# Another order of the first loads in front of a gated MLP: one part of a weight matrix ahead of the second unit's queries and keys, four parts behind later values

## The chip, the cores and the metric

The kernel runs on one core of a Trainium2 chip. The metric is the device time of one execution in microseconds (us); lower is better. TensorE (PE) multiplies matrices, VectorE (DVE), ScalarE (ACT) and GpSimd (POOL) do elementwise work, and nearly all transfers are issued by SyncE (SP). Every engine works through its own list of instructions in order, and an instruction that waits holds up all that stands behind it on that engine.

## What is computed

Chunked attention over 4 batches, 8 heads, 768 tokens and a head dimension of 64, followed by a gated MLP with a product over the tokens:

```
for each chunk of 32 queries:                      # 24 chunks
    k_ctx, v_ctx = keys, values from 16 before the chunk to 8 behind it
    k_full, v_full = 8 memory rows + k_ctx, v_ctx
    a = softmax(q_c @ k_full.T / 8)
    x_c = a @ v_full
x  : (4, 768, 512)                                 # heads side by side
h  = relu(x @ w_in);  u, v = h[..., :512], h[..., 512:]
vn = (v - mean(v)) / sqrt(var(v) + 1e-6)
vs = einsum('ts,bsd->btd', w_spatial, vn) + b_spatial
out = (u * vs) @ w_out
```

All inputs are 32-bit floats but w_in and w_out, which are 64-bit floats in memory.

## The kernel before

**Units.** The attention is done in 24 units: a unit is four chunks (128 queries) of all heads of one batch, six units to a batch. Unit i needs its queries and keys (loaded for two units at a time by `load_qk(g)`; the first pair is loaded as two single units, `load_qk(0, (0,))` and `load_qk(0, (1,))`), a copy of its keys with the memory keys between them (`prep`, ACT, L404), and its values (`load_v(i)`, four transfers, each with 128 KB or 96 KB). `burst(i)` holds 64 small matmuls for the scores of unit i ("s", L419 `sx<-kmain,q`) and 64 for the product of unit i-1's probabilities with its values ("a", L419 `sx<-vmain,pT`). The softmax is three steps on DVE with an exp on ACT between: maximum (L476), subtract (L480), exp (L485), sum and reciprocal (L490 to L493). The probabilities are transposed on PE (L507) and copied (L510), the output of "a" is scaled on DVE (L459, `xs`), transposed on PE (L523, `xt`), and split into a high part (ACT, L528) and a low part (DVE, L532), the tile x.

**First product.** Each product is made of three matmuls, high times high, low times high and high times low. w_in has 512 rows (four parts of 128, c = 0 to 3) and 1024 columns in two halves: the u half (part 0) and the v half (part 1). `w_in_part(c, part, rank, load_rank, engine)` loads one such part, 512 KB of 64-bit numbers, into one of four buffers (`big`), makes 32-bit numbers of it (`from_f64`: ACT L864 and L869, DVE L873 and L874, POOL L879), and splits these into `win_h` (ACT L893) and `win_l` (L897, on DVE for the v parts and on POOL for the u parts). `ffn_v` of unit t's 128 tokens takes x of this unit and the four v parts, in order of c (L561 to L563, 128x512); `ffn_u` takes x of three units and the four u parts (L561 to L563, 128x384). So no `ffn_v` can end before all v parts are split, and no `ffn_u` before all u parts are. Results go to DRAM (`vn_far`, `u_far`) and come back for the second half of the kernel, the spatial product and the product with w_out (L710).

**Who sets the order.** Nobody writes out the order of the engines' lists. Each step is given to `Plan.op` with its engine, an assumed duration, what it reads and writes, and a rank. `Plan.order` then plays through the whole kernel by these assumed durations: of all steps that could go, the one with the earliest start is taken, on equal start the lower rank. The result is the fixed order of each engine's list. A transfer is taken to land at `max(pipe, issue) + size * drag / rate` plus `landing`, with `pipe` the end of the transfer before it: so `landing` and `drag` change no transfer, but they change when the plan believes its data to be there, and with that the order of all lists. Loads with `seq=True` keep the order of the program on SP. `alone` keeps a DVE step off planned POOL work and POOL off it. Where PE would wait in the plan between 9 and 36 us, small matmuls that nobody reads (L252, `idle`) are put in, as many as fit.

**How many transfers fly.** `held_by` sets a wait of each transfer on an earlier one, in the plan as in the kernel, so that no more than a window of megabytes is under way (and, after the first 9 MB, no more than 8 transfers): 2.0 MB for the first 9 MB, 1.2 MB up to 38 MB (`MIDDLE`), 1.75 MB behind that.

Of the kernel before, what the change touches and what calls it, by code (L numbers as in the profile page):

```python
# [10 lines left out]
U32 = mybir.dt.uint32  # L11
# [8 lines left out]
SLOT = 40  # L20
LEFT = 16
WIN = 64
MIDDLE = (38.0, 1.2)
PIECES = 4
NEG = -1.0e30

# [1 line left out]
class Plan:  # L28
# [14 lines left out]
    def op(self, eng, us, fn, r=(), w=(), rank=0.0, mb=0.0, tail=0.0, after=None, alone=False, drag=1.0, shared=False):  # L43
        n = len(self.ops)
        deps, begun = set(), set()
        if after is not None:
            begun.add(after)
        for key in r:
            deps.add(self.writer.get(key))
            self.readers.setdefault(key, []).append(n)  # L50
        for key in w:
            deps.add(self.writer.get(key))
            deps.update(self.readers.get(key, ()))
            self.writer[key], self.readers[key] = n, []
        deps -= {None, n}
        held = {k[:2] for k in (*r, *w) if isinstance(k, tuple) and k[0] in self.rings}
        for s in held:
            if s not in self.slots and s[0] not in self.loose:
                if s[0] in self.newest:
                    begun.add(self.newest[s[0]])  # L60
                self.newest[s[0]] = n
            self.slots.setdefault(s, []).append(n)
        begun -= deps
        self.ops.append((eng, us, fn, deps, rank, mb, tail, held, begun, alone, drag, shared))
        return n
# [74 lines left out]
    def held_by(self, flight, mb, none):  # L140

        moved = sum(size for _, size in flight)
        window = self.early[1] if moved <= self.early[0] else MIDDLE[1] if moved < MIDDLE[0] else self.window
        for back, (name, size) in enumerate(reversed(flight), 1):
            mb += size
            if back == 8 and moved > self.early[0] or mb > window:
                return name
        return none
# [10 lines left out]
def tile_chunked_attention_gmlp(  # L159
# [43 lines left out]

    sizes = {"f": 3, "sx": 1, "pt": 1, "xt": 1, "y": 5, "st": 9, "big": 4, "uo": 2, "x": 2, "vm": 3,
             "q": 2, "k": 2, "kT": 2, "p": 1, "xs": 1, "pT": 1, "vr": 2, "op": 4, "sm": 2, "ug": 6, "ot": 11}
    plan = Plan(sizes, {"f", "y", "st", "big", "ot"}, rate=0.30, landing=2.5, lat=0.06, window=1.75, early=(9.0, 2.0))
    op = plan.op

    def act(n):
# [56 lines left out]
    def src(t, offset, ap):  # L266
        return bass.AP(tensor=t.tensor, offset=offset, ap=ap)
# [12 lines left out]
    def transfer(e, out_, in_, mb, of=None):  # L280
        ins = e.dma_start(out=out_, in_=in_)
        made.setdefault(of, []).append(ins.ins.name)
        wait = plan.held_by(flight, mb, None)
        if wait:
            wait_for(ins, [wait], "pace")
        flight.append((ins.ins.name, mb))

    def load(dst, src_, w, rank, r=(), eng="SP", slow=1.0, us=0.45, seq=False, drag=1.0, of=None):
        e = {"SP": nc.sync, "ACT": nc.scalar, "POOL": nc.gpsimd}[eng]
        n = 4  # L290
        for s in src_.shape:
            n *= s
        mb = n / 1e6 * slow
        n = op(eng, us, lambda: transfer(e, dst() if callable(dst) else dst, src_, mb, of), r=r, w=w, rank=rank, mb=mb,
               after=line.get(eng) if seq else None, drag=drag)
        if seq:
            line[eng] = n
# [10 lines left out]
    def spot(name, g, shape):  # L308
        if (name, g) not in t_:
            alloc(name, g, shape, F32)  # L310
        return t_[name, g]

    def load_qk(g, units=(0, 1), seq=True):
        i = 2 * g
        b, c0 = i // UB, (i % UB) * UC
        off = b * H * D * S + c0 * CH
        nk = 2 * UT + CH
        lo = LEFT if c0 == 0 else 0
        hi = nk - LEFT if c0 + 2 * UC == NC else nk
        q0, q1 = units[0] * UT, units[-1] * UT + UT  # L320
        k0, k1 = max(lo, q0 + (CH if q0 else 0)), min(hi, q1 + CH)
        u = units[0]
        ks = ("k", g)
        n = PIECES if g > 1 else 1
        for t in range(n):
            ts = slice(t * T // n, (t + 1) * T // n)
            load(lambda ts=ts: spot("q", g, [P, T, 2 * UT])[:, ts, q0:q1],
                 src(q, off + q0 + ts.start * P * S, [[S, P], [P * S, T // n], [1, q1 - q0]]), w=[("q", g, u, t)], rank=10.0 * i,
                 slow=1.15, seq=seq)
        for t in range(n):  # L330
            ts = slice(t * T // n, (t + 1) * T // n)
            load(lambda ts=ts: spot("k", g, [P, T, nk])[:, ts, k0:k1],
                 src(k, off - LEFT + k0 + ts.start * P * S, [[S, P], [P * S, T // n], [1, k1 - k0]]), w=[("k", g, u, t)],
                 rank=10.0 * i, slow=1.15, seq=seq)

        def pad():
            a = t_["k", g]
            if k0 == lo > 0:
                nc.gpsimd.memset(a[:, :, 0:lo], 0.0)
            if k1 == hi < nk:  # L340
                nc.gpsimd.memset(a[:, :, hi:nk], 0.0)
        if k0 == lo > 0 or k1 == hi < nk:
            op("POOL", 0.2, pad, w=[ks + (u, "pad")], rank=10.0 * i, after=len(plan.ops) - 1)
# [203 lines left out]
    seq = [0]  # L547
# [305 lines left out]
    def from_f64(name, src_, rank, load_rank, home, after=()):  # L853
        big = ("big", *name)
        zk = ("st", ("z", name))

        def get():
            a = alloc("big", big, [P, 2 * DH], U32).rearrange("p (c w) -> p c w", w=2)
            t_[big] = a
            return a  # L860
        load(get, src_.bitcast(U32).rearrange("p (c w) -> p c w", w=2), w=[("big", big)], r=after, rank=load_rank, seq=True)

        def scale_():
            nc.scalar.activation(alloc("st", ("z", name), [P, DH], F32), t_[big][:, :, 1].bitcast(F32), AF.Copy,  # L864
                                 scale=2.0 ** -112)

        def rest():
            a = t_[big][:, :, 0]
            nc.scalar.activation(a, a, AF.Copy, scale=2.0 ** -29)  # L869

        def shift():
            zu = t_["st", ("z", name)].bitcast(U32)
            nc.vector.tensor_scalar(zu, zu, 3, None, op0=ALU.logical_shift_left)  # L873
            nc.vector.scalar_tensor_tensor(zu, t_[big][:, :, 1], 0x80000000, zu,  # L874
                                           op0=ALU.bitwise_and, op1=ALU.bitwise_or)

        def add():
            zu = t_["st", ("z", name)].bitcast(U32)
            nc.gpsimd.tensor_tensor(t_[big][:, :, 1] if home else zu, zu, t_[big][:, :, 0], op=ALU.add)  # L879
        op("ACT", 0.66, scale_, r=[("big", big)], w=[zk], rank=rank)  # L880
        op("DVE", 1.12, shift, r=[("big", big)], w=[zk], rank=rank, alone=True)
        op("ACT", 0.66, rest, r=[("big", big)], w=[("big", big, "r")], rank=rank)
        op("POOL", 1.6 if home else 1.35, add, r=[("big", big, "r"), zk] if home else [("big", big, "r")],
           w=[("big", big)] if home else [zk], rank=rank)
        if home:
            return (lambda: t_[big][:, :, 1].bitcast(F32)), ("big", big)
        return (lambda: t_["st", ("z", name)]), zk
# [14 lines left out]
    def w_in_part(c, part, rank, load_rank, sub_eng):  # L902
        cols = slice(part * DH, (part + 1) * DH)
        z, zk = from_f64(("win", c, part), w_in[c * P:(c + 1) * P, cols], rank, load_rank, False)
        split(sub_eng, DH, lambda x: (win_l if x else win_h)[:, c, cols], z, [zk], [("win", c, part)], rank)
# [64 lines left out]
    for j in range(NV):  # L970
        spread_mem(j, "DVE" if j < 1 else "POOL", 1.0 + 10 * j)
    load_qk(0, (0,))
    load_qk(0, (1,))
    w_in_part(0, 1, 5.0 + 0, 2.0 + 0, "DVE")
    w_in_part(1, 1, 5.0 + 1, 2.0 + 1, "DVE")
    w_in_part(2, 1, 5.0 + 2, 2.0 + 2, "DVE")
    w_in_part(3, 1, 5.0 + 3, 2.0 + 3, "DVE")
    load_v(0)
    load_qk(1)
    w_in_part(0, 0, 25.0 + 0, 15.0 + 0, "POOL")  # L980
    load_v(1)
    w_in_part(1, 0, 25.0 + 1, 15.0 + 1, "POOL")
    load_v(2)
    w_in_part(2, 0, 25.0 + 2, 15.0 + 2, "POOL")
    w_in_part(3, 0, 25.0 + 3, 15.0 + 3, "POOL")
    for j in range(NK):
        spread_keys(j, 1.0 + j)
    for i in range(NU + 1):
# [23 lines left out]
    for b in range(B + 1):  # L1012
        if b < B:
            rank = 300.0 + 10 * b
# [67 lines left out]
```

## Time and profile before

| | |
|---|---|
| three timed runs | 376.54, 379.18, 381.41 us (median 379.18) |
| profiled execution | 375.05 us, span 373.3 us from the first to the last instruction |
| PE busy in the span | 355.9 us (95%) |
| DVE, ACT, POOL busy | 285.0 (76%), 187.1 (50%), 160.5 us (43%) |
| granted TensorE clock, mean | 0.999 of full speed |

The busy time of PE holds the filling matmuls of L252, which are no work of the kernel. The stretches below are in us from the start of the span. A row of the timeline gives start, duration, engine, line, operation, the tile written and the tiles read, and how many; brackets give the engine's idle time before it and what ended that.

### The profile page before, as it was taken

To read this page: it belongs to the slowest core of one execution; us is meant where nothing else is said; L and a number is where in the kernel's file an instruction comes from. 1 tells how busy PE (TensorE), PEld (TensorE's weight loads), DVE (VectorE), ACT (ScalarE), POOL (GpSimd) and SP (SyncE) were. 2 spreads that over 40 slices of the span, in tenths; PEclk is the share of its full clock that TensorE was granted. 3 is DMA by queue.
4 is the path that set the end of the run, shared out by engine and by line. 5 is a ranking of instruction groups with operands and counts; after the bars stand their busy time and mean duration, and the time that the engine had idled before them with its cause. 6 is when DMAs were issued, how large, how long until landed. Compare 5 with 4: busy or idle time off the path is not lost.

```text
span 373.3 us, 11922 instructions
## 1 busy us (share of the span) xinstructions
PE 355.9 (95%) x4988; PEld 326.7 (88%) x4988; DVE 285.0 (76%) x479; ACT 187.1 (50%) x334; POOL 160.5 (43%) x155
## 2 busy tenths in 40 slices
PE   2987989999999999999999999999999999999995
PEld 2865877998988978979889898999999999999995
DVE  3888856748758568566598589999969896898893
ACT  3768435454555454554473355346434743744371
POOL 6446642374386077520042194961256025106500
PEclk9999999999999999999999999999999999999999
DMA  8995888778787765886742648205720662230014
GB/s 230 316 260 140 232 257 210 235 217 220 228 251 214 249 212 147 274 232 194 216 163 93 246 137 311 88 2 173 246 90 3 207 217 84 84 130 2 0 54 159
DMA packets 48517, 65.52 MB, mean 176 GB/s; under 512 B 5456, under 2 KB 39888, under 8 KB 48464
## 3 DMA queue, kind: packets, MB, share of 16 engines
q1 hardware_dynamic: 47808, 64.44, 56.5%
q8 instruction: 39, 0.64, 0.8%
q10 hardware_dynamic: 656, 0.33, 0.3%
q14 instruction: 14, 0.11, 0.1%
HBM read 45.88 MB, written 18.87 MB: 173 GB/s over the span
## 4 chain that ended last, share of the span: by engine, by line
PE 83%; DVE 11%; ACT 2%; issue 2%; DMA 1%; SPq 0%; ACTq 0%; DVEq 0%
PE y L710 21%; PE f L710 15%; PE f L561 12%; PE f L562 11%; PE f L563 11%; PE sx L419 9%; PE xt L523 3%; PE pt L507 3%; DVE op L690 2%; DVE sm L673 2%; DMA k<-in_k_dram 1%; DVE st L874 1%; DVE st L873 1%; DVE wout L897 1%; DVE p L480 1%
## 5 line engine op out<-in xcount | busy, mean ns | idle before, releaser
L710 PE MATMUL y<-wsp,op 128*128 128x384 f32 x288 | 52.0, 336 | 0.9 <-ACT st L750 0.9
L764 POOL TENSOR_TENSOR ug<-st,ug 128x384 f32<-128x384 f32 x24 | 36.0, 1513 | 38.4 <-DVE st L756 34.4
L710 PEld LDWEIGHTS y<-wsp,op 128*128 128x128 f32 x288 | 49.9, 188 | 1.2 <-ACT st L750 1.2
L561 PE MATMUL f<-x,win_h 128*128 128x384 f32 x128 | 46.1, 360 | 0.0
L563 PE MATMUL f<-x,win_h 128*128 128x384 f32 x128 | 43.2, 337 | 0.0
L562 PE MATMUL f<-x,win_l 128*128 128x384 f32 x128 | 43.1, 337 | 0.0
L561 PE MATMUL f<-win_h,x 128*128 128x512 f32 x96 | 40.8, 425 | 0.0
L710 PE MATMUL f<-wsp,op 128*128 128x384 f32 x216 | 39.4, 336 | 0.0
L562 PE MATMUL f<-win_h,x 128*128 128x512 f32 x96 | 37.9, 394 | 1.0 <-DVE x L532 1.0
L563 PE MATMUL f<-win_l,x 128*128 128x512 f32 x96 | 37.7, 392 | 0.0
L710 PEld LDWEIGHTS f<-wsp,op 128*128 128x128 f32 x216 | 37.6, 188 | 0.0
L690 DVE TENSOR_TENSOR op<-sm,op 128x768 fp32r<-128x768 f32 x32 | 34.7, 1093 | 3.1 <-ACT op L687 2.6
L710 PE MATMUL y<-wout,op 128*128 128x256 f32 x288 | 35.9, 281 | 0.5 <-DVE op L690 0.5
L459 DVE TENSOR_TENSOR xs<-sx,rec 128x512 f32<-128x512 f32 x24 | 16.5, 687 | 25.1 <-PE sx L419 25.0
L710 PEld LDWEIGHTS y<-wout,op 128*128 128x128 f32 x288 | 34.7, 188 | 1.0 <-DVE op L690 0.8
L770 POOL TENSOR_TENSOR st<-st,bias 128x384 f32<-128x384 f32 x14 | 18.6, 1337 | 37.2 <-ACT st L750 28.4
L597 POOL TENSOR_TENSOR rstd<-ve,mhalf 128x1 f32<-128x1 f32 x24 | 14.7, 611 | 44.7 <-DVE ve L593 43.6
L687 ACT CAST op<-sm 128x768 fp32r<-128x768 f32 x32 | 26.2, 837 | 11.6 <-DVE sm L673 10.2
L419 PEld LDWEIGHTS sx<-kmain,q 64*32 64x32 f32 x1536 | 17.0, 107 | 14.8 <-issue 11.7
L622 ACT ACTIVATE uo<-f 128x384 f32<-128x384 f32 x32 | 15.6, 492 | 25.2 <-PE f L563 21.9
L398 POOL COPY vmain<-memv 8x1024 f32<-8x1024 f32 x22 | 23.9, 1090 | 10.0 <-PE sx L419 7.8
L419 PE MATMUL sx<-kmain,q 64*32 64x64 f32 x1536 | 20.9, 228 | 7.3 <-ACT kmain L404 7.0
(86 smaller groups left out, 770.6 us busy)
## 6 DMA issues: line engine op xcount, KB each, us to landing
vmain<-in_v_dram SPq DMA_DIRECT2D x48, 128.0 KB
vn_far<-st SPq DMA_DIRECT2D x24, 256.0 KB
u_far<-uo SPq DMA_DIRECT2D x32, 192.0 KB
vr<-vn_far SPq DMA_DIRECT2D x8, 768.0 KB
ug<-u_far SPq DMA_DIRECT2D x16, 384.0 KB
q<-in_q_dram SPq DMA_DIRECT2D x40, 128.0 KB
vmain<-in_v_dram SPq DMA_DIRECT2D x47, 96.0 KB
out_dram<-ot SPq DMA_DIRECT2D x33, 128.0 KB
```

The lines of the kernel that those rows point to most:

```text
L398: ins = {"DVE": nc.vector, "POOL": nc.gpsimd}[eng].tensor_copy(to, of)
L419: ins = nc.tensor.matmul(o, w_, m, start=True, stop=True, skip_group_check=True)
L459: nc.vector.tensor_tensor(xs.rearrange("p t r d -> p r t d"), t_["sx", i][:, :, 1], rec.rearrange("p t r -> p r t").unsqueeze(3).broadcast ...
L561: nc.tensor.matmul(o, lh, rh, start=(j == 0), stop=False)
L562: nc.tensor.matmul(o, ll, rh, start=False, stop=False)
L563: nc.tensor.matmul(o, lh, rl, start=False, stop=(j == len(pairs) - 1))
L622: op("ACT", act(HT), lambda: nc.scalar.activation(alloc("uo", i, [P, HT], F32), t_["f", n], AF.Relu), r=[("f", n)], w=[("uo", i)], rank=rank)
L687: nc.scalar.copy(half(0), of())
L690: nc.vector.tensor_tensor(half(1), of(), half(0).bitcast(F32), op=ALU.subtract)
L710: nc.tensor.matmul(o, x, y, start=first and m == 1, stop=m == 3 * chunks, skip_group_check=True)
L764: nc.gpsimd.tensor_tensor(g, t_[st(x)], g, op=ALU.mult)
L770: {"DVE": nc.vector, "POOL": nc.gpsimd}[eng].tensor_tensor(a, a, bias[:, 1], op=ALU.add)
```

## The change

Six edits. (1) The v part c = 1 of w_in is loaded ahead of the second unit's q and k; the other v parts follow behind these, now in the order 0, 3, 2. (2) The u parts, before one ahead of `load_v(1)`, one ahead of `load_v(2)` and two behind it, now stand two ahead of `load_v(2)` (1, then 0) and two behind it (3, then 2), so the first one goes behind the second unit's values. (3) The rank of the u parts' conversion is 12 + c for 25 + c. (4) The plan takes a transfer to land 2.0 us behind its last byte for 2.5. (5) It takes the 64-bit loads (w_in and w_out) to need 0.8 of the time. (6) Between 9 and 10.5 MB the window is 1.75 MB for 1.2.

```diff
-MIDDLE = (38.0, 1.2)
+MIDDLE = (10.5, 38.0, 1.2)
...
-        window = self.early[1] if moved <= self.early[0] else MIDDLE[1] if moved < MIDDLE[0] else self.window
+        window = self.early[1] if moved <= self.early[0] else MIDDLE[2] if MIDDLE[0] < moved < MIDDLE[1] else self.window
...
-    plan = Plan(sizes, {"f", "y", "st", "big", "ot"}, rate=0.30, landing=2.5, lat=0.06, window=1.75, early=(9.0, 2.0))
+    plan = Plan(sizes, {"f", "y", "st", "big", "ot"}, rate=0.30, landing=2.0, lat=0.06, window=1.75, early=(9.0, 2.0))
...
-        load(get, src_.bitcast(U32).rearrange("p (c w) -> p c w", w=2), w=[("big", big)], r=after, rank=load_rank, seq=True)
+        load(get, src_.bitcast(U32).rearrange("p (c w) -> p c w", w=2), w=[("big", big)], r=after, rank=load_rank, seq=True, drag=0.8)
...
     load_qk(0, (0,))
+    w_in_part(1, 1, 5.0 + 1, 2.0 + 1, "DVE")
     load_qk(0, (1,))
     w_in_part(0, 1, 5.0 + 0, 2.0 + 0, "DVE")
-    w_in_part(1, 1, 5.0 + 1, 2.0 + 1, "DVE")
+    w_in_part(3, 1, 5.0 + 3, 2.0 + 3, "DVE")
     w_in_part(2, 1, 5.0 + 2, 2.0 + 2, "DVE")
-    w_in_part(3, 1, 5.0 + 3, 2.0 + 3, "DVE")
     load_v(0)
     load_qk(1)
-    w_in_part(0, 0, 25.0 + 0, 15.0 + 0, "POOL")
     load_v(1)
-    w_in_part(1, 0, 25.0 + 1, 15.0 + 1, "POOL")
+    w_in_part(1, 0, 12.0 + 1, 15.0 + 1, "POOL")
+    w_in_part(0, 0, 12.0 + 0, 15.0 + 0, "POOL")
     load_v(2)
-    w_in_part(2, 0, 25.0 + 2, 15.0 + 2, "POOL")
-    w_in_part(3, 0, 25.0 + 3, 15.0 + 3, "POOL")
+    w_in_part(3, 0, 12.0 + 3, 15.0 + 3, "POOL")
+    w_in_part(2, 0, 12.0 + 2, 15.0 + 2, "POOL")
```

## Rows read from the trace of the kernel before

**Rows 1.** Busy time of each engine by stretch: first PE, later DVE; last the clock.

```profile
7.00:24.20 17.20, 16.06 (x311) 12.76 (x311) 15.43 (x26) 11.24 (x20) 8.76 (x7) 1.00 1.04 310
24.20:37.40 13.20, 10.92 (x234) 8.14 (x232) 11.44 (x23) 10.01 (x18) 7.02 (x6) 1.00 0.64 173
37.40:54.50 17.10, 16.20 (x326) 14.08 (x327) 11.52 (x24) 6.32 (x12) 8.95 (x13) 1.00 0.85 246
54.50:203.00 148.50, 147.67 (x3025) 129.26 (x3023) 104.26 (x219) 77.78 (x138) 65.28 (x72) 1.00 0.72 213
```

**Rows 2.** Groups by line on PE, 7 to 37.4 us: the filling matmuls.

```profile
L252 PE MATMUL idle<-ident 128*128 128x256 f32 x44 | 11.9, 420 | 0.0
```

**Rows 3.** Timeline of PE, 6 to 38 us.

```profile
10.93 0.86 PE L419 MATMUL sx<-kmain,q 64*32 64x64 f32 x64
...
12.21 5.78 PE L252 MATMUL idle<-ident 128*128 128x256 f32 x26
...
18.36 0.86 PE L419 MATMUL sx<-vmain,pT 64*32 64x64 f32 x64
...
24.16 0.50 PE L561 MATMUL f<-win_h,x 128*128 128x512 f32 x1
...
27.13 0.86 PE L419 MATMUL sx<-vmain,pT 64*32 64x64 f32 x64
...
31.99 0.75 PE L419 MATMUL sx<-vmain,pT 64*32 64x64 f32 x51 [0.96 <-issue]
...
37.40 0.50 PE L562 MATMUL f<-win_h,x 128*128 128x512 f32 x1 [1.01 <-DVE x L532]
```

**Rows 4.** Timeline of DVE, 10 to 39 us.

```profile
10.55 0.69 DVE L490 TENSOR_REDUCE den<-p 128x8 f32<-128x512 f32 x1 [0.70 <-ACT p L485]
...
15.86 1.52 DVE L873 TENSOR_SCALAR st<-st 128x512 uint32<-128x512 uint32 x1
...
...
18.48 1.67 DVE L874 SCALAR_TENSOR_TENSOR st<-big,st 128x512 uint32<-128x512 uint32 x1
...
20.68 0.68 DVE L459 TENSOR_TENSOR xs<-sx,rec 128x512 f32<-128x512 f32 x1
...
22.86 0.68 DVE L532 TENSOR_TENSOR x<-xt,x 128x512 fp32r<-128x512 f32 x1
...
27.58 0.69 DVE L490 TENSOR_REDUCE den<-p 128x8 f32<-128x512 f32 x1 [0.76 <-ACT p L485]
...
32.80 0.69 DVE L459 TENSOR_TENSOR xs<-sx,rec 128x512 f32<-128x512 f32 x1 [0.69 <-PE sx L419]
33.40 0.68 DVE L476 TENSOR_REDUCE mx<-sx 128x8 f32<-128x512 f32 x1
34.00 1.08 DVE L601 TENSOR_SCALAR st<-st,mvar,rstd 128x512 f32<-128x512 f32 x1
35.00 0.42 DVE L873 TENSOR_SCALAR st<-st 128x512 uint32<-128x512 uint32 x1
35.45 0.69 DVE L874 SCALAR_TENSOR_TENSOR st<-big,st 128x512 uint32<-128x512 uint32 x1
...
38.27 0.42 DVE L873 TENSOR_SCALAR st<-st 128x512 uint32<-128x512 uint32 x1
```

**Rows 5.** Timeline of ACT: the key copy of the second unit.

```profile
8.15 0.72 ACT L404 COPY kmain<-k 128x640 f32<-128x640 f32 x1 [1.28 <-DMA k<-in_k_dram]
```

**Rows 6.** Transfers by stretch of one us: last column GB/s.

```profile
5.00:6.00 1.00, 1.00 1.27 168
...
7.00:8.00 1.00, 1.00 1.07 375
```

**Rows 7.** Timeline of SP, the queue that issues the loads.

```profile
16.65 2.54 SPq L281 DMA_DIRECT2D vmain<-in_v_dram  x4
...
35.11 0.35 SPq L281 DMA_DIRECT2D vn_far<-st  x1
35.51 1.87 SPq L281 DMA_DIRECT2D q<-in_q_dram  x4
```

## Prediction

> **What bounds the kernel now.** I read the busy time by stretch first. From 54.5 to 203 us PE is busy in 147.67 of 148.5 us, and from 37.4 to 54.5 us in 16.20 of 17.10 [rows 1]. There is next to nothing to win behind 37.4 us: whatever the plan reorders there, PE has work all the time, and the order of it doesn't change its sum. In front of 37.4 us it looks as busy (16.06 of 17.20 us, 10.92 of 13.20), but the second view, PE's groups by line, takes that back: 11.9 us of it are the filling matmuls of L252 that nobody reads [rows 2]. So the time of this kernel is the time at which PE gets an unbroken supply, plus a remainder that doesn't move. That point is the low part of x of the third unit: behind 1.01 us of waiting for it PE starts at 37.40 us and stands still no more for data [rows 3]. Whatever brings this point forward by one us, with PE's real work in front of it unchanged, is worth one us.
>
> Third view, PE's timeline: the scores of the second unit stand at 10.93, the first "a" at 18.36 behind 26 filling matmuls, the first w_in matmul at 24.16, the second "a" at 27.13, the third at 31.99 us [rows 3]. Fourth, DVE in the same time: 15.43 us busy of 17.20, then 11.44 of 13.20 [rows 1]. The first "a" was done by 19.22 us (18.36 + 0.86), but DVE came to scale it only at 20.68, because the conversions of w_in stood in front; x of the first unit was complete at 23.54 (22.86 + 0.68) [rows 3, 4]. So up to 24 us the list of DVE is the bound, not a landing. Between 24 and 37 us it is mixed: DVE waits 0.76 us for an exp and 0.69 us for the third "a" [rows 4]. The second "a" was free to go long before 27.13: its values had been issued from 16.65 on, the last of four by 19.19 (16.65 + 2.54) [rows 7]. It stands late because the plan believed in a late landing.
>
> **The change part by part.** The transfers themselves are the same bytes and the same number of instructions: eight w_in parts, conversions of four instructions on ACT and DVE and POOL each and the split. Nothing is removed or added but waits; everything is an order.
>
> *The v part ahead of the second unit's q and k.* 0.524 MB now go in front of them. At the rates of the stretch, 375 GB/s down to 168 [rows 6], that delays q and k by 1.4 to 3.1 us. The key copy ran at 8.15 straight from the landing [rows 5]; it would run between 9.6 and 11.3, and the scores 0.8 us later, at 10.4 to 12.1. They ran at 10.93, behind fillers [rows 3]. I take the rate of the later row, since the part would come just when the queue has filled: 1.4 to 1.6 us, so no loss; at the other end 1.2 us. In return the conversion of the first part can start in DVE's gap of 0.70 us at 10.55 [rows 4]: one shift and combine (0.42 + 0.69 = 1.11 us, the pair at 35.00 [rows 4]) fills it. Gain **0.7**, bounds 0 and 0.7.
>
> *The other v parts, 0, 3, 2.* Only a swap of names: the part that lands last is used third and no longer fourth. A group of `ffn_v` takes 2.97 us for four steps (27.13 - 24.16 [rows 3]), so the fourth part had to be there 2.2 us behind the first matmul and the third 1.5; x comes later than the parts, so zero, and 0.7 us at most if x came that much earlier.
>
> *The landing of 2.0 us and the factor 0.8.* They move no byte. Worked through by the code's own formula (its belief, used for the order alone), the first unit's values now "land" some 2.4 us and the second's some 4 us earlier. So fewer fillers stand in front of the first "a", and the second "a" moves from behind the first `ffn_v` group to its beginning. The first of these is worth nothing by itself: DVE is still working on the v parts when it ends. The second is worth what DVE idles in 24 to 37 us: 0.76 + 0.69 = **1.45 us** [rows 4]. Bounds: 0 (the gaps come back elsewhere, since an exp between two DVE steps always leaves some) and 1.45. PE's own 0.96 us at 31.99 [rows 3] is put down to no wait that can be moved; it stays.
>
> *What DVE does before x of the third unit and needn't.* At 33.40 the maximum of the fourth unit (0.68), at 34.00 the normalising of the first v tile (1.08, slowed) stand before it [rows 4]. With the second and third "a" earlier they can fall behind. I take 1.0 us of these 1.76; bounds 0 and 1.76.
>
> *The u parts with rank 12.* This goes the other way. Before, ranks of 25 put them behind the second and third unit (20, 30); three of the four u shifts were done before x of the third unit, the fourth at 38.27 [rows 4]. With rank 12 and earlier belief all four go first: one more pair, **+1.1 us**; bounds 0 and 1.1 + 1.0, the second being one collision with a POOL step. For a shift took 1.52 us where the clean one took 0.42, and a combine 1.67 for 0.69 [rows 4]; in such times POOL was adding. The u parts aren't needed before the first `ffn_u`, behind 40 us, so moving one behind `load_v(1)` costs nothing; its cover is the `ffn_v` work, 2.97 us a unit.
>
> *The window of 1.75 MB and SP.* Before, the next q load stood behind a store on SP until 35.51 us, because that store waited for a tile [rows 7]. In the new window the plan can put these loads ahead of the store. They are wanted behind 40 us, where PE lacks only 0.9 of 17.1 us [rows 1]: zero, at most 0.9. Behind that, landing and 0.8 reorder the w_out conversions too, under a PE that is full: ±0.5.
>
> Sum: -0.7 - 1.45 - 1.0 + 1.1 = **-2.05 us**, from 375.05 of the profiled execution to 373.0. That execution was below all three timed runs; on their median the same step is 379.18 - 2.05 = 377.1.
>
> **The rivals.** *No gain.* DVE has the same work in front of the third unit's x, and its list is 87 to 90% full [rows 1]; a gap filled at one exp opens at the next. For it speaks that xs waited on DVE and not DVE on it at 20.68 [rows 4]; against it that two gaps are plain waits for steps put late. 379.2 us.
>
> *Slower: the u parts crowd out the third unit.* Place: DVE from 25 to 37 us. By rank 12 each u shift goes ahead of any attention step of units 2 and 3 that is ready with it, and each POOL step of a u part (the add, the subtraction) now lies beside the fullest stretch of DVE. Price: one pair more, 1.1, and two more collisions at 1.1 and 1.0 (1.52 - 0.42, 1.67 - 0.69) [rows 4], together 3.2, with gains of 0.7 and half of 1.45 beside: +1.8, 381.0 us. It decides once more than one further collision falls before x of the third unit. [...]
>
> *More than that.* The collisions of before (1.1 + 1.0, and 0.6 of the slowed normalising, 1.08 against the 0.42 of the like shift) vanish as the new order happens to lie: 2.7 us more of the same stretch, and the deferral reaches 1.76: -5.5, 373.7 us. Two of the three collisions sit between v parts [rows 4], whose landing order changes, so it can be.
>
> *The change doesn't do what it says.* If "landing" is now too short, the plan believes in data that isn't there and an in-order list waits. On the early loads the cover is large (last value issued by 19.19, used at 27.13 [rows 3, 7]), and this case falls into "no gain".
>
> **How the numbers follow.** Forecast 377.1 with a chance of 0.40, its own range 375.3 to 378.5. No gain, 379.2, 0.25. Slower, 381.0, 0.15. More, 373.7, 0.20. The median of three runs may itself be off by about 2 us, by their spread of 376.54 to 381.41. To leave out no more than 2 in 10, the range goes from 372.6 to 381.2. A measurement of this kernel tells about 2%, 7.6 us, from no change. Faster by over 2% (below 371.6) needs the largest case and a low sample: 0.09; slower by over 2% (above 386.8): 0.02; within: 0.89.
>
> **What would show it.** In the changed kernel: the fillers of L252 below 11.9 us; the second "a" some 3 to 4 us before 27.13, and the third before 31.99; the first w_in matmul within 1 us of 24.16, because DVE still sets it; DVE's gap of 0.70 before the first reciprocal chain filled by a shift; PE's last wait for x of the third unit about 2 us before 37.4; all four u shifts before it; q loads of the third pair on SP around 30 us. Behind 54.5 us PE's busy share unchanged. The prediction is wrong if the point of unbroken supply moves and the end doesn't (then PE loses it again later), if the first w_in matmul moves by over 2 us (then a landing or the plan's fillers were the bound and not DVE), or if PE has new gaps behind 60 us from the reordered lists.

## The result and the profile after

The changed kernel takes 382.15 us (median of 22 runs, 377.1 to 386.0), the kernel before 376.57 us (22 runs, 374.79 to 381.41), so the medians lie 5.6 us apart. The ratio is 1.0112, 95% interval 1.0084 to 1.014, which is 4.2 us: it counts fast runs alone, those within 1.5% of the fastest of their kernel, and that leaves out nine of the 22 after. The forecast was 2 us faster; by either measure it came out slower, and the median lies outside the range of the prediction, 372.6 to 381.2 us. The profiled execution after took 377.1 us (span 375.3, clock 0.999) against 375.05 (373.3, 0.999), and it is the fastest of the 22; its trace alone would have hidden most of the loss. So a second profile, of another execution of the same kernel, was needed (the first experiment).

The stretches of after, as [rows 1] (PE first, DVE third; the last three columns are the clock, the busy share of the DMA engines and GB/s):

```profile
7.00:24.20 17.20, 15.35 (x287) 11.88 (x269) 13.97 (x26) 11.22 (x19) 7.98 (x7) 1.00 1.01 266
24.20:37.40 13.20, 11.74 (x236) 8.91 (x235) 11.37 (x21) 9.68 (x17) 5.45 (x6) 1.00 0.98 245
37.40:54.50 17.10, 16.56 (x330) 14.01 (x331) 13.92 (x30) 9.95 (x19) 11.72 (x15) 1.00 0.86 235
54.50:203.00 148.50, 145.36 (x3003) 125.64 (x3002) 103.97 (x215) 74.56 (x132) 63.54 (x70) 1.00 0.72 208
```

Two things stand out against [rows 1]: in 54.5 to 203 us, where nothing was to change, PE is busy 145.36 us for 147.67; and the transfers of 7 to 24.2 us move 266 GB/s for 310 with all 16 engines busy (share 1.01).

PE's timeline of after, 10 to 59 us, as [rows 3]:

```profile
10.60 1.17 PE L419 MATMUL sx<-kmain,q 64*32 64x64 f32 x64 [0.87 <-DVE st L874]
...
18.37 0.86 PE L419 MATMUL sx<-vmain,pT 64*32 64x64 f32 x64
...
23.97 0.50 PE L561 MATMUL f<-win_h,x 128*128 128x512 f32 x1
...
25.59 0.85 PE L419 MATMUL sx<-vmain,pT 64*32 64x64 f32 x64
...
31.04 0.87 PE L419 MATMUL sx<-vmain,pT 64*32 64x64 f32 x64 [0.46 <-DMA vmain<-in_v_dram]
...
37.74 0.66 PE L507 MATMUL pt<-ident,p 128*128 128x128 f32 x4 [1.11 <-ACT p L485]
...
42.88 0.45 PE L561 MATMUL f<-x,win_h 128*128 128x384 f32 x1
...
58.12 0.35 PE L419 MATMUL sx<-vmain,pT 64*32 64x64 f32 x17 [1.53 <-issue]
```

The second and third "a" did move ahead (27.13 to 25.59, 31.99 to 31.04), but the wait for x of the third unit at 37.40 became one for an exp at 37.74. A point that both kernels pass is the first matmul of `ffn_u` (the first L561 of 128x384): 41.48 us before, 42.88 after. After has one score burst of 0.79 us in front of it that before has behind it, so on equal work it is 42.09: **0.6 us later, where 2.05 us earlier was forecast**.

What took the gain, as I read the trace: ACT waits six times for a part of w_in, 5.7 us in all (1.62, 1.65, 0.42, 0.41, 0.37 and 1.23), where before has no such wait. The first and the last in ACT's timeline of after:

```profile
8.09 0.67 ACT L864 ACTIVATE st<-big 128x512 f32<-128x512 f32 x1 [1.62 <-DMA big<-in_moe_w_in_dram]
...
34.49 0.68 ACT L864 ACTIVATE st<-big 128x512 f32<-128x512 f32 x1 [1.23 <-DMA big<-in_moe_w_in_dram]
```

and DVE's behind it, as [rows 4]:

```profile
35.21 0.43 DVE L873 TENSOR_SCALAR st<-st 128x512 uint32<-128x512 uint32 x1 [0.89 <-ACT st L864]
...
36.28 0.68 DVE L480 TENSOR_TENSOR p<-sx,mx 128x512 f32<-128x512 f32 x1
36.88 0.68 DVE L532 TENSOR_TENSOR x<-xt,x 128x512 fp32r<-128x512 f32 x1
...
39.03 0.38 DVE L873 TENSOR_SCALAR st<-st 128x512 uint32<-128x512 uint32 x1
```

The plan put a u part where it believed it landed; it landed later. ACT waits for it until 34.49 and DVE's in-order list waits 0.89 us for ACT. Behind that wait stand the subtraction whose exp PE then waits for (36.28) and x of the third unit, which ends at 37.56 (36.88 + 0.68); before it ended at 37.34. No run isolates this chain. In the second profile of the same kernel, below, ACT's waits for w_in come to 3.1 us only, and the first `ffn_u` matmul is as late.

### The profile page after: what moved, and what is told of

The parts are those of the page before. It is cut to its first block, busy times and chain, and to the rows that moved or that the text cites. A ratio compares the mean times of both kernels' runs of the same rounds, so it can differ in the third digit from the quotient of the medians.

```text
span 375.3 us, 11925 instructions
## 1 busy us (share of the span) xinstructions
PE 357.6 (95%) x4982; PEld 326.9 (87%) x4982; DVE 286.2 (76%) x479; ACT 188.3 (50%) x334; POOL 156.7 (42%) x155
## 4 chain that ended last, share of the span: by engine, by line
PE 78%; DMA 11%; DVE 5%; issue 2%; ACT 2%; SPq 1%; ACTq 0%; DVEq 0%
PE y L710 22%; PE f L710 15%; PE f L561 10%; PE f L563 10%; PE f L562 9%; PE sx L419 7%; DMA big<-in_moe_w_in_dram 5%; DMA big<-in_moe_w_out_dram 3%; PE xt L523 2%; PE pt L507 2%; DMA q<-in_q_dram 2%; DMA k<-in_k_dram 2%; SPq L281 1%; DVE op L690 1%; DVE xs L459 1%
## 5 line engine op out<-in xcount | busy, mean ns | idle before, releaser
L764 POOL TENSOR_TENSOR ug<-st,ug 128x384 f32<-128x384 f32 x24 | 34.1, 1436 | 36.2 <-DVE st L756 28.8
L561 PE MATMUL f<-x,win_h 128*128 128x384 f32 x128 | 46.1, 360 | 0.0
L561 PE MATMUL f<-win_h,x 128*128 128x512 f32 x96 | 41.1, 429 | 0.2 <-issue 0.2
L770 POOL TENSOR_TENSOR st<-st,bias 128x384 f32<-128x384 f32 x14 | 17.7, 1275 | 40.6 <-ACT st L750 29.1
L710 PE MATMUL f<-wout,op 128*128 128x256 f32 x216 | 27.2, 280 | 0.0
```

The source lines that it names most:

```text
L561: nc.tensor.matmul(o, lh, rh, start=(j == 0), stop=False)
L710: nc.tensor.matmul(o, x, y, start=first and m == 1, stop=m == 3 * chunks, skip_group_check=True)
L764: nc.gpsimd.tensor_tensor(g, t_[st(x)], g, op=ALU.mult)
L770: {"DVE": nc.vector, "POOL": nc.gpsimd}[eng].tensor_tensor(a, a, bias[:, 1], op=ALU.add)
```

## The experiments

Each ratio is against the kernel before, timed on the same chip; "clock" is the mean granted clock of the executions.

**The changed kernel, unedited, profiled once more.**

> The changed kernel once more, unedited, for a second trace. Theory A (the new order and the shorter belief make the in-order lists wait for the w_in parts and the values, so the unbroken supply of PE comes no earlier): span near 375 to 378 us at a granted clock of 0.999, PE's wait for x of the third unit again ends between 37.3 and 38.5 us. Theory B (most of the 1.1% is a lower granted clock of TensorE in some stretch): most executions are at a mean granted clock of 0.986 to 0.995 and 378 to 386 us, and the trace, if it catches one, shows a stretch of some 10 us at half the clock.

386.61 us, ratio 1.0281 (1.0188 to 1.0374); profiled 387.17 us, span 385.4, clock 0.986. So it was as theory B had it, a lower granted clock. PE's timeline, three of its bursts:

```profile
59.20 0.35 PE L419 MATMUL sx<-vmain,pT 64*32 64x64 f32 x17 [2.63 <-issue]
...
118.34 0.45 PE L419 MATMUL sx<-vmain,pT 64*32 64x64 f32 x10 [2.73 <-issue]
...
175.80 0.21 PE L419 MATMUL sx<-vmain,pT 64*32 64x64 f32 x1 [2.53 <-issue]
```

In the middle of a burst, which waits for nothing between its matmuls, PE stands still for over 2.5 us; "issue" says that no semaphore held it. The stretches behind two of these (third column from the end: the clock):

```profile
58.00:60.00 2.00, 0.80 (x20) 0.70 (x20) 0.32 (x1) 0.00 (x0) 0.33 (x1) 1.00 0.70 225
60.00:62.00 2.00, 2.00 (x10) 1.64 (x8) 1.84 (x4) 0.00 (x0) 1.75 (x2) 0.58 0.07 22
62.00:64.00 2.00, 2.00 (x7) 1.60 (x6) 1.13 (x3) 1.50 (x3) 0.00 (x0) 0.56 0.00 0
64.00:66.00 2.00, 2.00 (x12) 1.69 (x11) 0.84 (x4) 0.87 (x2) 0.00 (x0) 1.00 0.58 148
...
176.00:178.00 2.00, 2.00 (x7) 1.58 (x7) 1.92 (x3) 0.00 (x0) 0.00 (x0) 0.59 0.62 180
178.00:180.00 2.00, 2.00 (x9) 1.67 (x8) 0.85 (x3) 1.20 (x3) 0.00 (x0) 0.55 0.08 14
```

Behind each of the three stalls the granted clock is 0.55 to 0.59 in two stretches of 2 us, though PE is busy in them from the stall's end on; then it is back at 1.00. The account then closes. PE's busy time is that of one stretch, from the first `ffn_u` matmul to the end, less the extra burst of 0.79 us in before; the idle time is the rest of that stretch:

| us | before | after, profiled first | after, profiled again |
|---|---|---|---|
| first `ffn_u` matmul, equal work | 41.48 | 42.09 (+0.61) | 42.03 (+0.55) |
| PE idle behind it | 7.05 | 7.46 (+0.41) | 13.21 (+6.16) |
| PE busy behind it | 323.98 | 324.96 (+0.98) | 329.37 (+5.39) |
| span | 373.3 | 375.3 (+2.0) | 385.4 (+12.1) |

The three stalls sum to 7.89 us, against 1.42 before: +6.47 of idle time. The two stalls of before, in PE's timeline:

```profile
53.42 0.32 PE L419 MATMUL sx<-vmain,pT 64*32 64x64 f32 x8 [0.90 <-issue]
...
136.95 0.31 PE L419 MATMUL sx<-vmain,pT 64*32 64x64 f32 x6 [0.52 <-issue]
```

The six stretches of 2 us with a clock of 0.55 to 0.59 lose 2 x (1 - clock) each, 5.1 us together (an estimate from these clocks): most of the 5.39 us of busy time. So 11.55 of 12.1 us lie where the prediction saw "next to nothing".

**Where the stalls sit.** I number PE's instructions in the trace from the first on: two to a row of PE (a weight load and a multiplication), and one for each of its semaphore instructions, which the views leave out (104 with the drains in the changed kernel). A full burst, "s" and "a", is 128 rows, 256 instructions, in 1.41 us.

| trace | stalls in the "a" of | left to do | instruction | less a multiple of 256 |
|---|---|---|---|---|
| before | 3rd, 5th, 16th unit | 51, 8, 6 | 961, 1730, 5313 | 193, 194, 193 |
| again | 3rd, 6th, 13th, 20th | 40, 17, 10, 1 | 962, 1985, 4290, 6593 | 194, 193, 194, 193 |

All stand at the same count within 256. The trace also shows what comes in such steps (the transfers by queue, the execution profiled again):

```profile
q8 instruction: 39, 0.64, 0.7%
```

39 packets of 16.4 KB (0.64 MB / 39). PE's 4982 rows twice, 9964, and the 104 make 10068 instructions, and these hold 39 places with a count of 193 above a multiple of 256. One packet began to move 2.4 to 2.7 us before PE went on from each of the three (at 56.64 for 59.20, 115.61 for 118.34, 173.35 for 175.80). So, as I read it, PE stands at the end of a packet of 256 instructions whose successor isn't there yet. At 35 of the 39 places no idle time is put down to issue; at four it is, with up to 2.73 us, where a burst uses 256 instructions in 1.41 us.

This also tells what the length of a stall is made of. In the first profile of after PE stood at the same instruction as at 175.80 (6593), but shortly:

```profile
167.00 0.21 PE L419 MATMUL sx<-vmain,pT 64*32 64x64 f32 x1 [0.26 <-issue]
```

Its packet had begun to move at 164.65, 2.09 us before PE stopped at 166.74; in the second profile it began at 173.35, when PE had stopped at 173.27. In all nine such stalls of the table and of the first profile after, PE goes on 2.4 to 2.7 us after the packet began. So a stall is short where the packet set off early; why it sets off early in one execution and late in the next stays open.

**Half of the change at a time**: first the order of loads and the u parts' rank alone, then landing, factor and window alone.

```diff
 # order only: before.py with the new order of w_in_part lines and 12.0 + c; landing, drag, MIDDLE as before
 # belief only: after.py with the order of loads and 25.0 + c of before
```

> Only the order of the loads and the rank of the u parts are changed; landing 2.5, factor 1 and the windows are as before. Theory A (the belief is what makes lists wait): same as before within 0.4%, since the plan still counts on late landings. Rival (the order itself costs, by the delay of the second unit's q and k or by the u parts ahead of the third unit): 0.5 to 1.2% slower, like the whole change.

> Only landing 2.0, factor 0.8 and the windows are changed; the loads go in the old order with the old ranks. Theory A: 0.5 to 1.2% slower than before, ACT's waits for w_in parts between 8 and 36 us add up to 4 us or more, where the kernel before shows none. Rival (the order itself costs): same as before within 0.4%.

1.0315 (1.0225 to 1.0404) and 1.0199 (1.0116 to 1.0283), where the whole change had 1.0281 on the same chip: each half alone loses about as much as both together. Either theory expected one of the two runs to be the same as before, so both fall: ACT's waits for parts of w_in come to 3.75 us in order only, with the old belief, and to 2.6 us in belief only. In order only, PE's timeline:

```profile
40.20 0.66 PE L507 MATMUL pt<-ident,p 128*128 128x128 f32 x4 [2.88 <-ACT p L485]
...
87.91 0.32 PE L419 MATMUL sx<-vmain,pT 64*32 64x64 f32 x9 [2.48 <-issue]
```

The 2.48 us stand at count 194 again, 9 matmuls before the end of the 9th "a" (instruction 3010). Behind the 2.88 the clock is 0.54 and 0.61 from 42 to 46 us; behind the 2.48 it stayed at 1.00. The first `ffn_u` matmul stands at 47.47 us in order only and at 46.62 in belief only, so these two lose several us early, a stretch at a lower clock included (0.50 to 0.67 from 38 to 46 us in belief only). No single edit carries the loss: each re-plan has its own early waits and its own stalls.

**Moving the packets' ends.** n tiny matmuls that nobody reads, four instructions each, at the very start, shift every later instruction's number. Theory F says that PE stands still where a packet of 256 ends shortly before the end of a burst, and that the time goes with the number of such places.

```diff
+    def lead(n):
+        for m in range(n):
+            c, r = m % 4, 0
+            rows = slice(r * D, (r + 1) * D)
+            nc.tensor.matmul(idle[c * CH:(c + 1) * CH, r, 0:D], ident[rows, c * CH:(c + 1) * CH], ident[rows, 0:D],
+                             start=True, stop=True, skip_group_check=True)
...
+        lead(27)   # in the kernel before: 27, 60; in the changed kernel: 44, 32
         plan.emit()
```

> The kernel before with 27 tiny matmuls that nobody reads ahead of PE's first scores, where PE idles; the plan and everything else are unchanged. They are 108 instructions on PE (a weight load and a matmul, twice each). [...] In the traces so far all stalls put down to issue ended at instruction 193 or 194 of a packet. With 108 more the ends of bursts that lie 0 to 36 instructions behind such a point are those of the 11th and 18th 'a' instead of the 5th, 9th, 16th and 23rd: 373 to 376 us, stalls, if any, in the 11th and 18th. Rival R (the time of the changed kernel is due to landings and new waits alone): unchanged against before within 0.3%, and no stall moves.

> As the run with 27, with 60 tiny matmuls (240 instructions). Theory F: the ends of the bursts that lie 0 to 36 instructions behind the end of a packet are now the 4th, 5th, 9th, 13th, 20th and 23rd, six in place of four: 379 to 386 us, like the changed kernel, with stalls in some of these. Rival R: unchanged against before within 0.3%, but for the time by which the tiny matmuls hold back the first scores (under 1.5 us).

> The changed kernel with 44 tiny matmuls ahead of PE's first scores (176 instructions). Theory F: the 3rd, 7th and 14th 'a' end 0 to 15 instructions behind the end of a packet in place of the 4th, 6th, 13th, 17th and 20th; two behind 40 us in place of four: 375 to 379 us, 4 us or more below the changed kernel. Rival R: like the changed kernel, 382 to 387 us.

> The changed kernel with 32 tiny matmuls (128 instructions). Theory F: the 8th, 11th, 15th, 22nd and 24th 'a' end 0 to 35 instructions behind the end of a packet: 381 to 388 us, as slow as the changed kernel or slower, with the stalls in these bursts and none in the 6th, 13th and 20th. Rival R: like the changed kernel, and like the one with 44.

1.0077 (1.0018 to 1.0135), 0.9988 (0.993 to 1.0046), 1.0192 (1.0152 to 1.0233) and 1.0026 (0.9966 to 1.0085); the medians of four executions each are 379.8, 374.85, 383.34 and 379.64 us, for 375.47 before. The last ratio says little, as it counts only 375.58 and 377.89 us of four, and the profiled execution took 383.12. The stalls moved to where the count puts a packet's end. Before with 27, PE's timeline:

```profile
98.48 0.30 PE L419 MATMUL sx<-vmain,pT 64*32 64x64 f32 x3 [1.30 <-issue]
...
154.03 0.32 PE L419 MATMUL sx<-vmain,pT 64*32 64x64 f32 x9 [0.21 <-issue]
```

After with 44 and after with 32, where the packet now ends at a burst's last matmul or right behind it:

```profile
35.03 2.87 PE L252 MATMUL idle<-ident 128*128 128x256 f32 x6 [2.61 <-issue]
...
123.53 0.24 PE L419 MATMUL sx<-vmain,pT 64*32 64x64 f32 x1 [2.36 <-issue]
```

```profile
100.19 0.45 PE L561 MATMUL f<-x,win_h 128*128 128x384 f32 x1 [2.52 <-issue]
...
157.41 0.48 PE L561 MATMUL f<-x,win_h 128*128 128x384 f32 x1 [2.61 <-issue]
```

And before with 60, which has none behind 40 us (the stretch of [rows 1] that was 147.67 busy):

```profile
54.50:203.00 148.50, 148.50 (x3032) 130.41 (x3031) 105.29 (x218) 77.70 (x139) 65.08 (x71) 1.00 0.74 215
```

The places hold: in every trace here but that of the tight run below, each stall over 0.7 us put down to issue behind 40 us ends at 193 or 194. The times expected didn't, in any of the four. I had counted each burst with a packet's end in its last part as a full stall, and before with 60 has six such places and no stall. In after with 44 the stall at 35.03, with a clock of 0.78, 0.50 and 0.87 from 34 to 40 us, is part of why the first `ffn_u` matmul comes at 46.43 us, 3.55 later than in after; that was not counted either. Rival R had the time right in two of the four (before with 60, after with 44), but it falls with the stalls that moved. Where a stall can be is shown; how long it gets can't be forecast from the place.

**No long bursts.** The "s" and "a" of units 6 to 23 are planned at least 2.85 us apart, in both kernels:

```diff
-        for what in (whole if split else [whole]):
+        apart = UB <= i < NU
+        first_half = None
+        for what in ("sa" if apart else whole if split else [whole]):
...
-            op("PE", us, lambda what=what: go(what), r=reads, w=writes, rank=rank, tail=0.25)
+            n = op("PE", us, lambda what=what: go(what), r=reads, w=writes, rank=rank, tail=0.25, after=first_half,
+                   gap=2.85 if first_half is not None else 0.0)
+            first_half = n if apart else None
```

> The kernel before, with the 64 small matmuls for the scores and the 64 for 'a' kept 2 us apart from the seventh unit on (some three steps of the MLP between them). Theory F (PE's instructions run out inside the double burst of 256): no stall put down to issue over 0.5 us behind 60 us, 371 to 375 us, and fewer executions above 377. Rival R (the stalls have to do with the transfers of the time, not with the double burst): stalls as before, 374 to 380 us.

> The changed kernel with the two bursts kept apart in the same way. Theory F: what the change costs behind 60 us goes away with the stalls: 372 to 377 us, within 1.5 us of the kernel before with its bursts apart, the rest being the 0.6 us by which the changed kernel reaches its first u product later. Rival R: 380 to 387 us, as the changed kernel.

1.0182 (1.0103 to 1.0261) and 1.017 (1.0102 to 1.0238), clocks 0.994 to 1.000 in all eight executions. Both times expected, 371 to 375 and 372 to 377 us, were too low by the price of the split bursts. Two bursts of 64 cost some 0.3 us more than one of 128 (2 x 0.86 against 1.41), 18 times: 5.4 of the 6.6 us that the kernel before loses by it (383.67 for 377.03). But between the two the 1.1% is gone (medians of 383.67 and 383.47 us, though both lists were planned anew): spans of 380.9 and 381.0 us, with after's first `ffn_u` matmul again 0.5 us later on equal work. The longest stalls left behind 60 us, in before and in after:

```profile
113.00 0.31 PE L419 MATMUL sx<-vmain,pT 64*32 64x64 f32 x5 [0.40 <-issue]
```

```profile
100.43 0.30 PE L419 MATMUL sx<-kmain,q 64*32 64x64 f32 x3 [1.00 <-issue]
```

**Which edit took the early gain.** The v part behind the second unit's q and k again (shown); or the old order and rank of the u parts, as in the kernel before.

```diff
     load_qk(0, (0,))
+    load_qk(0, (1,))
     w_in_part(1, 1, 5.0 + 1, 2.0 + 1, "DVE")
-    load_qk(0, (1,))
     w_in_part(0, 1, 5.0 + 0, 2.0 + 0, "DVE")
```

> The changed kernel, but with the v part c = 1 again behind the second unit's q and k (v order 1, 0, 3, 2); PE's list is the same but for one filler that stands elsewhere. Theory V (the part in front costs: it holds back q and k, and lowers the rate of the early transfers from 306 to 310 GB/s to 251 to 268): rate in 7 to 24.2 us again above 290 GB/s, the first u product up to 1.5 us earlier than the 42.1 us of the changed kernel (42.88 without the 0.79 us burst of scores that the kernel before has behind it). Rival U (the u parts ahead of the third unit cost): no change there. Both leave the stalls where the changed kernel has them, in the 'a' of the 6th, 13th, 17th and 20th unit, and the time at 380 to 387 us.

> The changed kernel with the old order and rank of the u parts (the first of them ahead of the second unit's values, ranks 25 + c); PE's list is that of the run in which only the belief was changed, but for one filler that stands elsewhere. Theory U: the first u product comes 1 us or more earlier than in the changed kernel. Theory V: it comes no earlier, but as late as in the run with the belief alone or later, 43 to 46 us. The time 380 to 387 us by either, as the stalls of PE's instructions stand where they do in the run with the belief alone.

1.0118 (1.0044 to 1.0192) and 1.0177 (1.009 to 1.0265). Their first `ffn_u` matmul is at 43.33 and 44.26 us, later than the change's 42.88. In the second of these the clock is 0.60 and 0.54 from 32 to 36 us, which costs some 1.7 us (an estimate from these two); without it, it would be 0.3 us ahead of the change, not 1 us or more. Neither edit alone hides an early gain; both theories fall. The early rates stay low too, 279 and 282 GB/s.

**Does other traffic set a stall's size?** The same lists, with only SP's waits changed from 10.5 to 46 MB: fewer transfers under way (4 and 0.6 MB), or more (16 and 2.4 MB), the latter in before as well.

> The changed kernel, unedited, as the measure for the next three on the same chip. The place of the stalls is settled (instruction 193 or 194 of a packet of PE's instructions, inside the 'a' of the 6th, 13th, 17th and 20th unit); their size is not: 0.3 and 2.5 us at the same place in two executions. Expected here by both theories: 379 to 387 us, stalls in these places alone.

> The changed kernel with fewer transfers under way between 10.5 and 46 MB: 0.6 MB and 4 transfers in place of 1.2 to 1.75 MB and 8. Only the waits that SP sets are changed; the lists of all engines are the same, and with them the places of the stalls. Theory Q (the packet of PE's instructions waits behind the data that are under way): the stalls in the 6th, 13th, 17th and 20th 'a' stay under 1 us, no half clock behind 60 us, 374 to 380 us, unless keys and values now come late, which shows as waits for DMA or ACT's key copy. Rival P (the packet is asked for late, whatever is under way): stalls and time as in the changed kernel.

> The changed kernel with more under way between 10.5 and 46 MB: 2.4 MB and 16 transfers. Theory Q: the stalls at the same places grow, 2.5 to 5 us each, with half clock behind most of them, 386 to 395 us. Rival P: as the changed kernel.

> The kernel before with the same looser pace (2.4 MB and 16 transfers between 10.5 and 46 MB, its lists unchanged). Theory Q: the stalls in its 5th, 9th, 16th and 23rd 'a' grow from 0.5 to 0.9 us to 2 us and more, and it loses the advantage over the changed kernel: 379 to 388 us. Rival P: as the kernel before, 374 to 378 us.

Unedited 1.0225 (1.0152 to 1.0298), from three executions of 383.06 to 387.15 us; the profiled one took 444.8 us at a mean clock of 0.756 and isn't counted. Tight 1.1518: PE waits seven times for 1.39 to 4.90 us on an exp; as I read it, the data come too late, and it tells nothing of the stalls. Loose 1.0257 (1.0177 to 1.0336) and 1.0029 (0.999 to 1.0067). PE's timeline of after, loose (its lines lie 7 further down):

```profile
57.55 0.35 PE L426 MATMUL sx<-vmain,pT 64*32 64x64 f32 x17 [1.81 <-issue]
...
171.39 0.21 PE L426 MATMUL sx<-vmain,pT 64*32 64x64 f32 x1 [2.25 <-issue]
```

The same instructions stall, by less than in the second profile of the unedited kernel (2.63 and 2.53 us) and by more than in the first (1.53 and 0.26), and the ratio is that of the unedited kernel; before, loose, stays in rival P's 374 to 378 us (377.6). That the transfers under way set the size isn't borne out.

## Why the prediction was wrong

**The step that failed most: "There is next to nothing to win behind 37.4 us: whatever the plan reorders there, PE has work all the time, and the order of it doesn't change its sum."** PE's list wasn't short of data there; as I read the traces, it was short of instructions, with up to 2.73 us at one place. The new order and landing times changed the number of fillers (44 to 38) and the order of everything behind, and so where in PE's list the 256-instruction steps end. In before PE stood still at three of these places, for 0.5 to 1.0 us; in after at up to four, for 0.26 to 2.73 us, differing by execution, and behind each of the three over 2.5 us some 4 us at a clock of 0.55 to 0.59 followed. The sign stood in the trace: "PE's own 0.96 us at 31.99 [rows 3] is put down to no wait that can be moved; it stays" was read as a constant, though its releaser is "issue". It is this stall, and it moved; the 0.90 and 0.52 us behind 37.4 stood in the same trace. Of the prediction's own signs of being wrong it is the last that came: "if PE has new gaps behind 60 us from the reordered lists". Over the executions: the 13 runs of after that the ratio counts have a median clock of 0.994, 33 of before beside the experiments 1.000; 0.006 of a span of 380 us is 2.3 of the 4.2 us (an estimate from these numbers), which leaves 1.9 us to the stalls themselves and the early 0.6.

**The early terms, -0.7, -1.45 and -1.0, together: +0.6 us measured.** Their parts came as told: the first shift fills DVE's gap (9.36 us), both "a" move ahead, though by 1.5 us where 3 to 4 were forecast for the second, the first matmul of w_in stays within 1 us (23.97), the next q loads go at 31.15. But "They move no byte" was taken to mean that a shorter landing is harmless, and the new order to cost no waits. ACT waited 5.7 us for parts of w_in that it hadn't waited for before, the third "a" 0.46 us for values, and DVE 0.89 us on ACT; the key load of the second pair went to SP's queue at 16.18 for 14.08. The shorter landing isn't the only source of these waits, as order only has 3.75 us of them without it; which of them costs the 0.6 us is not shown. That the plan believes in data that isn't there was the fourth rival, and it was filed under "no gain" at 379.2 with a cover read from the values alone, not from the w_in parts. The fillers fell in number, but in the first profile not in time: 38 take 12.0 us (10.3 in the second), against 11.9 [rows 2].

**The term +1.1 for the fourth u pair didn't come**: its shift still lies behind x of the third unit (39.03). The collisions of before, 1.52 and 1.67 us [rows 4] beside POOL's adds of 15.38 and 18.25 us, vanished (shifts 0.38 to 0.61, combines 0.69; a split at 13.99, beside POOL's add of 13.51, now took 1.37 us), which was the condition of the rival "more than that". It didn't pay; as I read the trace, because landings bound the stretch then.

**The slower rival, 381.0, had about the right time by luck, for the wrong reason.** The u parts don't crowd DVE; with their old order and rank the kernel is no faster.

**Open:** why the packet of instructions sets off early in one execution and late in the next (0.26 and 2.53 us at the same instruction); why the clock falls behind most long stalls and not behind some (2.46, 2.48 and 2.52 us without); why the early transfers move 238 to 290 GB/s in every version with an edit of the order or the belief, for 294 to 310 in the kernel before and its variants.

## What to carry to other kernels

An edit to a planner's inputs re-lays every list, so the place of the edit isn't the place of its cost: look at idle time marked "issue" in bursts of small matmuls before calling a full engine safe, and count its instructions, those on semaphores too, to the step at which the stalls lie, here 256. Profile a changed kernel more than once and compare the granted clocks of all its timed runs; the fastest execution showed 2 us of a loss that was 12 in another. A landing time in a plan is a claim about a loaded queue; test it by the waits for landings that the new lists show, part by part.

## What was not expected of the hardware

In these traces PE stood still for up to 2.9 us at the end of a step of 256 instructions that a burst of small matmuls (256 in 1.41 us) had reached, and the same instruction cost 0.26 us in one execution and 2.53 in another. Behind seven of the ten stalls of 2.3 us and more in these traces (that of the tight run not counted) the granted clock fell to 0.50 to 0.59 in a stretch of 2 us, though PE was busy in it; where it lasted some 4 us, it cost some 1.7 us more (an estimate from the two clocks of 0.58 and 0.56 behind the first stall of the second profile). It is not only stalls for instructions that this follows: in the run with the old u parts PE waited 1.64 us for ACT and 1.32 us for DVE just before 240 us, and the clock was 0.66 and 0.50 from 240 to 244 us; in order only the like two waits, 1.64 and 1.33 us, left it at 1.00.
